# Batch 6's key turn one step sooner, tile 6's token sums split around a PSUM sum, and GpSimd's last value-fold steps held behind them

## The chip, the cores and the metric

The kernel runs on one core of a Trainium2 chip. The metric is device time in microseconds of one execution. The kernel before took 225.37 us (median of three runs, 225.24 to 225.75). The engines are called by the profile's names: PE (matrix multiply), PEld (its weight loads), DVE (vector), ACT (scalar), POOL (GpSimd) and SP (the queue that issues most transfers late in the kernel). Each has a queue of its own, which it works through in program order; semaphores join them.

## The reference

```python
k_p = k.reshape(B, H, Sp, 8, D).mean(axis=3)        # B=8, H=8, S=576, D=64, Sp=72
v_p = v.reshape(B, H, Sp, 8, D).mean(axis=3)
attn = softmax(q @ k_p^T / sqrt(D))
x = (attn @ v_p) as 4608 tokens x 512
h = maximum(maximum(x @ w1, x @ w2), x @ w3)        # 512 -> 768
out = h @ w_out                                     # 768 -> 512
```

## The kernel before, in words

The maximum is taken as x·w1 + max(0, x·(w2-w1), x·(w3-w1)). The part x·w1·w_out is folded into one 512x512 matrix (`wm`), so that the two differences alone are multiplied out, and the output is x·wm + max(...)·w_out.

The work is laid out by batch and by tile. A batch (0 to 7) is 576 tokens of attention: GpSimd sums eight key rows and eight value rows into one, in three steps each (`fold_steps`, L163, L164, L166); PE turns the pooled keys into a PSUM tile `pkt` (`turn_k`, L201), from which four copies (L210) write the two key matrices `kz`, for batches over 2 two by DVE and two by ACT; PE makes scores (L220), ACT their exponentials (L225), PE multiplies with the pooled values in five chunks of 128 tokens (`values`, L270), and DVE divides each chunk (L276, L278). The chunk is then turned by a DMA transpose, issued from SP, into the token ring `xT` (`turn_x`, L255). A tile (0 to 8) is 512 tokens of that ring. Tile 6 is tokens 3072 to 3583: batch 5 from its token 192 on, and the first chunk of batch 6.

From tile 6 on, the hidden products are made from seven block products instead of eight (`seven`, L763). The tile's tokens are cut into two halves of tokens and two of channels, x0 to x3, and four sums of them are needed: T1 = x1-x0, T2 = x3-T1, T3 = x3-x1, T4 = x2-T2 (`fold_t`, L566). DVE makes them for tile 6, in four instructions of 128x512 elements, GpSimd for tile 7. Products 1 and 2 use x0 and x2, product 6 uses T2, product 5 T1, product 7 T3, product 4 T4. A product's result is copied from PSUM by ACT (L805) or added to a kept one by DVE (`plus`, L776: one operand from PSUM).

The order is written out by hand in strings of words. `MIDDLE[4]` (L907) is the middle stage with tile 4's output products, batch 5's value chunks and batch 6's keys; `block(5, LEAD, ...)` follows it, with tile 5's hidden products (L364) and batch 6's scores between them; then `ORDER` (L856) weaves the rest. In `MIDDLE[4]` a word such as `v4` is batch 5's value chunk 4, `x4` its transpose, `6:k` the turn of batch 6's keys, `3` or `2h` an output product (L721), `e5` and `e2` a DVE sum of it into the output (L734), and `k7+3` or `v7+3` three steps of a fold on GpSimd. In `ORDER`, `k7` is batch 7's key turn, `1a` product 1 for the first 128 hidden columns, `F` half an output tile (L414 or L418), `T` the token sums, `v62` batch 6's value chunk 2 and `s70` a piece of batch 7's scores. Every word puts its instructions on all the queues that it needs, so a word that moves, moves on each of them.

Buffers set waits too. The two scores of a piece need both key matrices. `psc`, `pav` and `pkt` share two PSUM slots in the middle stage; `pw` and the output products `oB` and `oC` share three. In the last stage `pkt`, `pB` and `psf` share two (`SC`), `pA` has two, `po` one and `val` one. Tile 6's sums are written to `pad`, whose memory is that of batch 7's value rows `vt`, which the fold's first step reads last. `held` with `gate` (L834) makes the next GpSimd step wait for a DVE instruction.

Of the kernel before, what the change touches and what calls it, by code (L numbers as in the profile page):

```python
# [10 lines left out]
ALU = mybir.AluOpType  # L11
# [3 lines left out]
def kernel(  # L15
# [46 lines left out]
    def psum(shape, dtype, name, tag, bufs):  # L62
        return pools[-1].tile(shape, dtype, name=name, tag=tag, bufs=bufs)
# [3 lines left out]
    def after(loads, first):  # L67
        for x in loads:
            tc.add_manual_dep(x.ins, first.ins.name, mybir.DependencyInfo(
                mybir.DependencyClass.Sync, mybir.DependencyReason.DATA),  # L70
                reason="weights first")

    def load_k(b, eng, dtype=F16, parts=1):
        pad = 0 if b == 0 else 32
        kts[b] = (const if b == 0 else ld).tile(
            [96, 6, POOL * D + pad], dtype, name=f"kt{b == 0}", tag=f"kt{b == 0}")[
                :, :, 0:POOL * D].rearrange("p i (j d) -> p i j d", j=POOL)
        src = k[b].rearrange("h s d -> (h s d)").rearrange(
            "(p i j d) -> p i j d", p=96, i=6, j=POOL)
        n = 6 // parts  # L80
        return [eng.dma_start(out=kts[b][:, i:i + n], in_=src[:, i:i + n])
                for i in range(0, 6, n)][-1]

    def load_v(b, eng, dtype=F16, cuts=(0, H)):
        if b == 0:
            vts[0] = ld.tile([96, 4096], dtype, name="vt0", tag="vt")[:, 0:3072].rearrange(
                "p (h i d) -> p h i d", h=H, i=6)
            src = v[0].rearrange("h (p i) d -> p h i d", i=6)
            return [eng.dma_start(out=vts[0][:, h:g], in_=src[:, h:g])
                    for h, g in zip(cuts, cuts[1:])][-1]  # L90
        vts[b] = ld.tile([Sp, H, POOL, D], dtype, name="vt", tag="vt")
        src = v[b].rearrange("h (sp j) d -> sp h j d", j=POOL)
        return [eng.dma_start(out=vts[b][:, h:g], in_=src[:, h:g])
                for h, g in zip(cuts, cuts[1:])][-1]
# [30 lines left out]
    for sign in (1, -1):  # L125
        nc.gpsimd.affine_select(
            out=pick, in_=pick, compare_op=ALU.is_ge, fill=0.0, base=7 * (sign < 0),
            pattern=[[sign, 6], [-8 * sign, 128]], channel_multiplier=6 * sign)
    for i in range(3):
        load_w(slice(256 * i, 256 * i + 256))  # L130
    nc.gpsimd.dma_start(
        out=wo_sb, in_=moe_w_out.rearrange("(jc p) c -> p jc c", p=128))
# [243 lines left out]
    def new_hT():  # L376
        return sb2.tile([128, JCH, NB], F16, name="hT", tag="hT")
# [178 lines left out]
    def halves(n):  # L556

        return {i: tokens(NB * n + HALF * (i % 2), NB * n + HALF * (i % 2) + HALF,
                          2 * (i // 2), 2 * (i // 2) + 2) for i in range(4)}

    def turns(n):
        return (pad3 if n % 2 else pad)[:, 0:4]

    def fold_t(e, x, t):
        for i, a, b in ((0, x[1], x[0]), (1, x[3], t[0]), (2, x[3], x[1]), (3, x[2], t[1])):
            e.tensor_tensor(out=t[i], in0=a, in1=b, op=ALU.subtract)  # L566

    def fold_x(n):

        x, t = halves(n), turns(n)  # L570
        late = n >= LAST - 1
        for part in ([slice(0, 1), slice(1, 2)] if late else [slice(0, 2)]):
            fold_t(nc.gpsimd if late else nc.vector,
                   {i: x[i][:, part] for i in x}, [t[:, i, part] for i in range(4)])
        return {f"T{i + 1}": t[:, i] for i in range(4)}

    LAST = TOK // NB - 1
    th, so_new, tt_all, gate, held = {}, [], [], [], []
# [184 lines left out]
    def seven(n):  # L763

        x, banks, done = halves(n), {}, set()
        low = pad4[:, 0:2]

        def kept(i, g):
            odd = (3 * n + g) % 2
            return (pad3[:, 4] if odd else pad2[:, 0]) if i == 1 else pad[:, 2 * (i - 3) + odd]  # L770

        def top(g):
            return pad4[:, 2:4] if (3 * n + g) % 2 else pad2[:, 1:3]

        def plus(out, i, g, p):
            nc.vector.tensor_tensor(out=out, in0=kept(i, g), in1=p, op=ALU.add)  # L776

        def best(row, c):
            nc.vector.scalar_tensor_tensor(
                out=hTs[n][:, row, :].rearrange("p (a c) -> p a c", a=2), in0=c[:, :, 0, :],  # L780
                scalar=0.0, in1=c[:, :, 1, :], op0=ALU.max, op1=ALU.max)

        def product(i, g):
            if i == 0:
                x.update(fold_x(n))
                return
            if not done:
                hTs[n] = (ld.tile([128, JCH, NB], F16, name="hT8", tag="ktFalse")
                          if n == LAST else new_hT())
            of = "B" if i == 2 else "C" if i in (4, 7) else "A"  # L790
            if i in FIRST:
                tag = {"A": PA, "B": SC, "C": BC}[of]
                banks[of, g] = psum([128, 2, HALF], F32, name=f"p{of}", tag=tag[0],
                                    bufs=tag[1])
            p = banks[of, g]
            for w in range(2):
                a, b = sw[w + 1][PRODUCTS[i][0]], x[PRODUCTS[i][1]]
                for kc in range(2):
                    mm = nc.tensor.matmul(p[:, w], a[:, kc, bass.ts(g, 128)], b[:, kc, :],  # L799
                                          start=(i in FIRST and w + kc == 0),  # L800
                                          stop=(w + kc == 2), skip_group_check=True)
            mms.append(mm)
            done.add((i, g))
            if i in (1, 6, 5):
                nc.scalar.copy(out=kept(i, g), in_=p)  # L805
            if i == 2:
                plus(top(g)[:, 0], 1, g, p)
            elif i == 3:
                nc.scalar.copy(out=top(g)[:, 1], in_=p)
                best(g, top(g))  # L810
            elif i == 4:
                plus(low[:, 0], 6, g, p)
                best(g + JH, low)
            elif i in (5, 7) and (12 - i, g) in done:
                plus(low[:, 1], 5, g, banks["C", g])

        return product
# [16 lines left out]
    def pool_step(n, name):  # L834

        what, b = name[0], int(name[1])
        if name[2:] == "<":
            load = {"k": lambda: load_k(b, nc.gpsimd), "v": lambda: load_v(b, nc.gpsimd),
                    "q": lambda: load_q(b)}[what]
            op = load()  # L840
            if what == "k":
                after([op], mms[-1])
            return
        if (what, b) not in folding:
            if what == "k":
                new_kp(b)
                folding[what, b] = fold_steps(nc.gpsimd, kts[b], kps[b])
            else:
                folding[what, b] = fold_steps(nc.gpsimd, vts[b], vp_all[:, b, :, 0:D])
        for _ in range(int(name[3:] or 3)):  # L850
            op = next(folding[what, b])
            for x in held:
                after([op], x)
            held.clear()

    ORDER = """  # L856
        k7 1a F F 2a T 1b v62 s70 F s71 s72 6a F s73 v63 5a 7a s74 s75 v64 F s76
        4a s77 3a s78 6b 2b 7b 1c v70 2c 5b T F 6c v71 3b F 5c 4b F v72 7c 3c 1a
        F 1b 4c v73 2a 2b 6b 6a F v74 5a 7a F 3a F T 1c 4a 5b 2c 6c 7b 3b F 5c
        4b F 1a 7c 2a 3c 6a 4c H 1b 2b 5a 6b 7a 3a h o1 1c 4a o2 5b 6c 7b 2c o6  # L860
# [3 lines left out]
    def weave():  # L864

        products, seen = {}, {}
        for name in ORDER.split():
            if name == "F":
                next(tiles)
            elif name == "H":  # L870
                fold_h(LAST - 1)
                outs = out_seven(LAST - 1)
            elif name == "h":
                fold_h(LAST - 1, True)
            elif name[0] == "o":
                outs(int(name[1]), 0, 1)
            elif name[0] in "ksvx":
                b = int(name[1])
                do(b, name[0] + name[2:])
                if name[0] == "v" and b > 2:  # L880
                    do(b, "x" + name[2:])
                if name[0] == "s" and name[2] == "4" and b + 1 < B:
                    do(b + 1, "T")
            else:
                n = seen[name] = seen.get(name, 5) + 1
                if n not in products:
                    products[n] = seven(n)
                products[n](*((0, 0) if name == "T" else
                              (int(name[0]), "abc".index(name[1]))))

    MIDDLE = {
        1: """
# [14 lines left out]
        4: """  # L907
            h k k7< q7< v7< h a1 a3 a2 a4 f ! v5+2 h h s0 h s1 h s2 h s3 h s4 b1 f ! k6+1 h s5
            h s6 h s7 h b2 b3 b4 f ! k6+2 v6+1
            1 v0 x0 2l v1 x1 7:T 6 7 v2 x2 5 v3 x3 e5 v4 x4 2h 3 6:k e2 4 v6+2 k7+3 v7+3  # L910
        """}
    folds = iter([f for wi in range(1, 3) for f in [fold_w(wi)] * 4])

# [81 lines left out]
```

## Time and profile before

| | |
|---|---|
| median of the runs | 225.37 us (225.24 to 225.75) |
| the profiled execution | 225.68 us |
| its span, first to last instruction | 224.0 us |
| PE busy | 214.2 us, 96% of the span |
| PEld, DVE, ACT, POOL busy | 146.6, 149.4, 122.4, 140.1 us |
| granted PE clock | 0.999 |
| chain that ended last | PE 86%, DVE 5%, DMA 3%, ACT 2% |

The profile is of one execution; its 224.0 us of span and 1.7 us around it make its 225.68 us. A row of the timeline has the start in us from the span's start, how long it lasts, engine, line, operation, output and inputs by the program's names, shape and how many instructions were merged; a bracket gives the idle time before it and what ended that. Matmuls are pipelined: a row's length holds the drain of its last one, so that the next row starts before it ends. A PE instruction's own share is read from the starts.

### The profile page before, as it was taken

How to read it: one execution, taken by the hardware profiler on the slowest of the kernel's cores; microseconds unless marked ns; L12 is line 12 of the kernel's file. 1: busy time of each engine (PE TensorE's matmuls, PEld its weight loads, DVE VectorE, ACT ScalarE, POOL GpSimd, SP SyncE). 2: the span in 40 equal slices, each digit the busy share in tenths (PEclk: the TensorE clock that was granted, in tenths of full speed). 3: DMA queues.
4: the chain of work that ended last, by engine and by line, in shares of the span. 5: the costliest groups of instructions: out<-in, count | busy, mean ns of one | idle time of the engine just before them, and what ended most of it. 6: DMA issues, size and time to landing. Idle time of an engine off the chain costs nothing.

```text
span 224.0 us, 4682 instructions
## 1 busy us (share of the span) xinstructions
PE 214.2 (96%) x1806; PEld 146.6 (65%) x1807; DVE 149.4 (67%) x292; ACT 122.4 (55%) x221; POOL 140.1 (63%) x111
## 2 busy tenths in 40 slices
PE   7688999999999999999999999999999999999993
PEld 2377744558755555875596569555587777788882
DVE  3558967037594395787479668727677786898840
ACT  2267534766875478237723862583876446554330
POOL 7975300999949977787768757999601903772020
PEclk9999999999999999999999999999999999999999
DMA  6999999989849999839999999764341523200266
GB/s 176 211 197 197 204 207 205 205 161 213 158 105 154 237 202 228 135 79 170 225 234 168 165 248 150 160 170 77 66 101 31 128 61 84 47 3 0 63 200 164
DMA packets 50710, 33.54 MB, mean 150 GB/s; under 512 B 27040, under 2 KB 46368, under 8 KB 50688
## 3 DMA queue, kind: packets, MB, share of 16 engines
q0 software_dynamic: 20304, 16.98, 48.3%
q1 hardware_dynamic: 29936, 15.87, 31.8%
q10 hardware_dynamic: 448, 0.39, 0.7%
q8 instruction: 14, 0.23, 0.5%
q14 instruction: 8, 0.07, 0.1%
HBM read 34.60 MB, written 9.44 MB: 197 GB/s over the span
## 4 chain that ended last, share of the span: by engine, by line
PE 86%; DVE 5%; DMA 3%; ACT 2%; issue 1%; SPq 0%; DVEq 0%; ACTq 0%
PE pw L364 26%; PE po L418 9%; PE oA L721 9%; PE pA L799 7%; PE psc L220 6%; PE po L414 5%; PE oC L721 4%; PE pav L270 4%; PE pC L799 4%; DMA ktTrue<-in_k_dram 3%; PE pm L351 2%; PE oB L721 2%; PE pxt L261 2%; PE pB L799 2%; PE pqt L194 1%; DVE xn L278 1%
## 5 line engine op out<-in xcount | busy, mean ns | idle before, releaser
L364 PE MATMUL pw<-xT,mw 128*128 128x512 f16 (+1 forms) x336 | 72.8, 348 | 0.3 <-ACT xT L264 0.2
L364 PEld LDWEIGHTS <-mw 128*128 128x128 f16 x336 | 31.6, 98 | 20.4 <-issue 0.6
L372 DVE TENSOR_TENSOR hT<-t,pw 128x512 f16<-128x512 f16 (+1 forms) x42 | 25.4, 610 | 23.2 <-ACT et L225 14.9
L225 ACT ACTIVATE et<-psc 72x576 f16<-72x576 f32 (+2 forms) x54 | 35.2, 661 | 6.7 <-PE psc L220 6.6
L163 POOL TENSOR_TENSOR half<-vt 72x2048 f32<-72x2048 f16 x7 | 28.4, 4059 | 13.7 <-DMA vt<-in_v_dram 13.3
L164 POOL TENSOR_TENSOR half<-half 72x1024 f32<-72x1024 f32 (+1 forms) x13 | 27.3, 2099 | 10.7 <-DVE rcp L276 6.1
L370 ACT ACTIVATE t<-pw 128x512 f16<-128x512 f32 (+1 forms) x42 | 22.6, 537 | 14.8 <-PE pw L364 14.3
L278 DVE TENSOR_TENSOR xn<-pav,rcp 128x512 f16<-128x512 f32 x40 | 27.7, 692 | 1.4
L220 PE MATMUL psc<-qT,kz 128*128 128x320 bf16 (+2 forms) x120 | 22.6, 278 | 1.3 <-DVE qT L196 0.9
L418 PE MATMUL po<-mwo,hT 128*128 128x512 f16 (+1 forms) x102 | 23.5, 366 | 0.0
L220 PEld LDWEIGHTS <-kz 128*128 128x128 bf16 x143 | 13.1, 98 | 13.8 <-ACT qT L196 1.1
L163 POOL TENSOR_TENSOR half<-ktFalse 96x1536 f32<-96x1536 f16 x6 | 18.8, 3131 | 4.0 <-issue 2.9
L805 ACT CAST pad<-pA 128x512 f16<-128x512 f32 x27 | 15.6, 588 | 7.4 <-PE pA L799 7.2
L566 POOL TENSOR_TENSOR pad<-xT 128x256 f16<-128x256 f16 x8 | 5.9, 738 | 20.8 <-ACT pad L805 12.2
L276 DVE RECIPROCAL rcp<-pav 128x8 f32<-128x8 f32 x40 | 8.2, 204 | 15.2 <-PE pav L270 14.9
L270 PEld LDWEIGHTS <-et 72*128 72x128 f16 x320 | 15.2, 98 | 3.5 <-issue 0.2
L731 ACT COPY osb<-oA 128x512 f32<-128x512 f32 x12 | 7.0, 586 | 18.2 <-PE oA L721 18.2
L414 PE MATMUL po<-wm,xT 128*128 128x512 f16 (+1 forms) x68 | 16.6, 366 | 0.0
L270 PE MATMUL pav<-vp,et 72*128 72x65 f16 x320 | 16.4, 194 | 0.1
L423 ACT COPY osb<-po 128x512 f32<-128x512 f32 (+1 forms) x16 | 9.2, 573 | 12.3 <-PE po L418 12.3
L799 PEld LDWEIGHTS <-sw 128*128 128x128 f16 x144 | 13.7, 98 | 3.0 <-issue 0.6
L776 DVE TENSOR_TENSOR pad<-pad,pC 128x512 f16<-128x512 f16 x18 | 12.3, 685 | 3.9 <-PE pC L799 3.6
(122 smaller groups left out, 383.4 us busy)
## 6 DMA issues: line engine op xcount, KB each, us to landing
out_dram<-osb SPq DMA_DIRECT2D x38, 128.0 KB, 5.2
ktFalse<-in_k_dram POOLq DMA_DIRECT2D x7, 576.0 KB, 8.4
qb<-in_q_dram POOLq DMA_DIRECT2D x7, 576.0 KB, 12.6
vt<-in_v_dram POOLq DMA_DIRECT2D x7, 576.0 KB, 16.7
mw<-in_moe_w_dram POOLq DMA_DIRECT2D x9, 256.0 KB, 9.4
out_dram<-osb SPq DMA_DIRECT2D x8, 256.0 KB, 6.1
ktTrue<-in_k_dram SPq DMA_DIRECT2D x3, 384.0 KB, 5.1
out_dram<-ob SPq DMA_DIRECT2D x8, 128.0 KB, 2.7
```

What stands on the lines that cost most here:

```text
L163: yield e.tensor_tensor(out=f, in0=t[:, :, 0:4, :], in1=t[:, :, 4:8, :], op=ALU.add)
L164: yield e.tensor_tensor(out=f[:, :, 0:2, :], in0=f[:, :, 0:2, :], in1=f[:, :, 2:4, :], op=ALU.add)
L220: nc.tensor.matmul(out, kz_all[b % 2][f % 2][rows, h, :], qTs[b][rows, n + i0:n + i1, 64 * (h % 2):64 * (h % 2) + 64], start=True, stop=True)
L225: nc.scalar.activation(out=out, in_=in_, func=FT.Exp, scale=1.0 / 64.0)
L270: nc.tensor.matmul(pav[:, h // 4, 65 * (h % 4):65 * (h % 4) + 65], ets[b][:, h, c0:c0 + 128], vp_all[:, b, h, :], start=True, stop=True)
L278: nc.vector.tensor_tensor(out=xn, in0=pv[:, :, :, 0:D], in1=rcp.to_broadcast([128, 2, 4, D]), op=ALU.mult)
L364: mm = nc.tensor.matmul(pw, w_sb[wi][:, kc, bass.ts(jc, 128)], x[:, kc], start=(kc == 0), stop=(kc == KCH - 1))
L372: nc.vector.tensor_tensor(out=hT[:, jc, c0:c1], in0=t, in1=pw, op=ALU.max)
L414: nc.tensor.matmul(po, tokens(128 * m, 128 * m + 128)[:, kc], wm_sb[:, kc, c], start=(kc == 0), stop=False)
L418: nc.tensor.matmul(po, hT[:, jc, bass.ts(mm, 128)], wo_sb[:, jc, c], start=False, stop=(jc == JCH - 1))
L721: nc.tensor.matmul(p, left, right, stop=(r == 4), skip_group_check=True, start=(i in FIRST and r == 0 and (m == 0 or n == LAST)))
L799: mm = nc.tensor.matmul(p[:, w], a[:, kc, bass.ts(g, 128)], b[:, kc, :], start=(i in FIRST and w + kc == 0), stop=(w + kc == 2), skip_grou ...
```

## The change

Two places of the written order are changed, and two helpers so that the token sums can be made in two parts.

- `MIDDLE[4]`: `v4 x4 2h 3 6:k` becomes `2h 6:k 3 v4 x4`. The key turn of batch 6 now stands ahead of output product 3 and of batch 5's value chunk 4; that chunk and its transpose stand behind product 3 and the stores which that product issues. `v7+3` at the end becomes `v7+1`.
- `ORDER`: `k7 1a F F 2a T 1b` becomes `1a k7 F F T 2a U 1b`. Product 1a stands ahead of batch 7's key turn. `T` makes only T1 and T2 for tile 6, ahead of product 2a and its `plus`; `U` makes T3 and T4 behind it. `U` then holds GpSimd's last two steps of batch 7's value fold (`v7+2`) until T4 is made.

```diff
-    def fold_t(e, x, t):
-        for i, a, b in ((0, x[1], x[0]), (1, x[3], t[0]), (2, x[3], x[1]), (3, x[2], t[1])):
-            e.tensor_tensor(out=t[i], in0=a, in1=b, op=ALU.subtract)
-
-    def fold_x(n):
+    def fold_t(e, x, t, which=(0, 1, 2, 3)):
+        for i in which:
+            a, b = ((x[1], x[0]), (x[3], t[0]), (x[3], x[1]), (x[2], t[1]))[i]
+            gate[:] = [e.tensor_tensor(out=t[i], in0=a, in1=b, op=ALU.subtract)]
+
+    def fold_x(n, rest):
 
         x, t = halves(n), turns(n)
         late = n >= LAST - 1
+        which = (0, 1, 2, 3) if late else (2, 3) if rest else (0, 1)
         for part in ([slice(0, 1), slice(1, 2)] if late else [slice(0, 2)]):
             fold_t(nc.gpsimd if late else nc.vector,
-                   {i: x[i][:, part] for i in x}, [t[:, i, part] for i in range(4)])
+                   {i: x[i][:, part] for i in x}, [t[:, i, part] for i in range(4)], which)
...
             if i == 0:
-                x.update(fold_x(n))
+                x.update(fold_x(n, g))
...
     ORDER = """
-        k7 1a F F 2a T 1b v62 s70 F s71 s72 6a F s73 v63 5a 7a s74 s75 v64 F s76
+        1a k7 F F T 2a U 1b v62 s70 F s71 s72 6a F s73 v63 5a 7a s74 s75 v64 F s76
...
-                products[n](*((0, 0) if name == "T" else
+                products[n](*((0, name == "U") if name in "TU" else
                               (int(name[0]), "abc".index(name[1]))))
+                if name == "U":
+                    held[:] = gate
+                    pool_step(n, "v7+2")
...
-            1 v0 x0 2l v1 x1 7:T 6 7 v2 x2 5 v3 x3 e5 v4 x4 2h 3 6:k e2 4 v6+2 k7+3 v7+3
+            1 v0 x0 2l v1 x1 7:T 6 7 v2 x2 5 v3 x3 e5 2h 6:k 3 v4 x4 e2 4 v6+2 k7+3 v7+1
```

## The prediction

> **What bounds the kernel now.** I read the page first: PE is busy for 96% of the span and holds 86% of the chain that ended last, at a granted clock of 0.999. A change that adds and removes no matmul can pay only where PE stands still. So I read the waits of the stretch that the change touches (130 to 180 us). Columns: who waited for whom, us in total, times, longest.
>
> ```profile
> PE pA L799 <- DVE pad L566: 0.5, 1, 0.5
> PE psc L220 <- ACT kz L210: 0.3, 1, 0.3
> DVE pad L776 <- ACT pad L805: 1.9, 2, 1.7
> ```
>
> PE waits twice: once for a token sum, once for a key copy. Next PE's timeline there, for the size of both.
>
> ```profile
> 142.62 0.30 PE L220 MATMUL psc<-qT,kz 128*128 128x320 bf16 x1
> 143.20 0.28 PE L220 MATMUL psc<-qT,kz 128*128 128x256 bf16 x1 [0.28 <-ACT kz L210]
> 144.18 0.41 PE L220 MATMUL psc<-qT,kz 128*128 128x320 bf16 x2
> 144.42 1.03 PE L364 MATMUL pw<-xT,mw 128*128 128x512 f16 x4
> ...
> 159.99 0.60 PE L220 MATMUL psf<-qT,kz 128*128 128x64 bf16 x6
> 161.07 0.60 PE L799 MATMUL pA<-pad,sw 128*128 128x256 f16 x4 [0.47 <-DVE pad L566]
> ```
>
> The brackets are too short, because a row's length holds its pipeline's drain. By starts, a pair of scores takes 144.42 - 144.18 = 0.24 us for 576 columns, so its first 320 take 0.13: the second score could have started at 142.76 and started at 143.20, a gap of **0.44**. The next pw group starts 0.86 to 0.87 us after a pw group of four 512-column matmuls, so the six score pieces (1024 columns) take 0.43: product 6a could have started at 160.42 and started at 161.07, a gap of **0.65**. Worked the same way, starts show no other gap of PE over 0.05 us from 100 us to its last matmul at 220. After 161.07 PE is thus the clock of the rest, and what it saves here it keeps, if no other engine is late.
>
> Then the engines that PE waited for: DVE, ACT and POOL.
>
> ```profile
> 140.52 0.69 DVE L278 TENSOR_TENSOR xn<-pav,rcp 128x512 f16<-128x512 f32 x1
> 141.12 0.96 DVE L210 COPY kz<-pkt 64x288 bf16<-64x288 bf16 x2
> 142.12 0.69 DVE L734 TENSOR_TENSOR osb<-osb,oB 128x512 f32<-128x512 f32 x1
> ...
> 158.59 0.69 DVE L776 TENSOR_TENSOR pad<-pad,pB 128x512 f16<-128x512 f16 x1 [1.70 <-ACT pad L805]
> 159.19 0.42 DVE L566 TENSOR_TENSOR pad<-xT 128x512 f16<-128x512 f16 x1
> 159.65 1.37 DVE L566 TENSOR_TENSOR pad<-xT,pad 128x512 f16<-128x512 f16 x1
> 160.94 0.41 DVE L566 TENSOR_TENSOR pad<-xT 128x512 f16<-128x512 f16 x1
> ```
> ```profile
> 142.18 0.96 ACT L210 COPY kz<-pkt 64x288 bf16<-64x288 bf16 x2 [0.86 <-DVE kz L210]
> ...
> 156.98 0.97 ACT L210 COPY kz<-pkt 64x288 bf16<-64x288 bf16 x2 [1.99 <-DVE kz L210]
> 157.97 0.59 ACT L805 CAST pad<-pA 128x512 f16<-128x512 f32 x1
> ```
> ```profile
> 152.77 4.06 POOL L163 TENSOR_TENSOR half<-vt 72x2048 f32<-72x2048 f16 x1
> 156.91 2.36 POOL L164 TENSOR_TENSOR half<-half 72x1024 f32<-72x1024 f32 x1
> 159.35 1.39 POOL L166 TENSOR_TENSOR vp<-half 72x512 f16<-72x512 f32 x1
> ```
>
> First gap: batch 6's key copies stand on DVE behind chunk 4's division; ACT's pair starts only when DVE's pair is done and ends at 143.14. Second gap: DVE stood idle for 1.70 us, because `plus` of 2a waited for ACT's cast of 1a, itself behind ACT's two key copies; the token sums stood behind `plus`; and T2 then took 1.37 where T3 and T4 took 0.41, while POOL's L166 ran (159.35 to 160.74).
>
> **The change, part by part.** No instruction is added or taken away; all are moved.
>
> *6:k ahead of 3 and v4.* On PE the three `pkt` transposes go from 140.53 to behind 2h: product 5 ends at 138.37, v3 takes 0.26, 2h 0.55, so 139.18. POOL's `kp` (137.66 for 0.99) is done at 138.65: cover of 0.5 us; each us later than that would stall PE. DVE's copies then follow e5's sum (139.69, next start 140.28) and end at 141.25; ACT's pair runs 141.3 to 142.3 instead of 142.18 to 143.14. The score that waited until 143.20 wants to start at 142.76: the gap of 0.44 closes, with 0.45 to spare. PE's order of 3, v4 and 4 keeps its sum.
>
> What is late next? On ACT the copy of product 3 now stands behind the key copies, 142.3 instead of 140.73; the relu copy behind it starts at 142.8 (143.16 before), its input being done at about 142.8. On DVE, chunk 4's division moves behind the key copies, so e2's sum of `oB` still starts at 142.12 and ends at 142.81; the second pw group takes oB's PSUM slot and, with the gap gone, wants to start at 142.86. That is the tightest place: the trace shows 0.05 us from a DVE end to PE's start (161.02 to 161.07). Bounds: no wait, or at the worst the whole 0.44 if DVE slips. I take 0, the nearest row being e2's own unchanged start. Scores s0 take `pkt`'s slot, free at 142.3, wanted at 142.62.
>
> On SP, the two stores of product 3 (0.68 each of the four that take 3.08, waits included) go ahead of x4, which is issued near 146.9 instead of 145.5. Its landing, 2.2 to 3.5 us after (rows of this stretch), is at about 150; T1 wants it at 157. Nothing, unless it takes 8 us more.
>
> *1a ahead of k7.* On PE 1a's 0.44 and the 0.13 of `pkt` change places. With PE 0.44 earlier, 1a ends at 155.05 and ACT casts it at 155.2 instead of 157.97; DVE's key copies end near 156.5, ACT's near 157.5. The first score of batch 7 takes `pkt`'s slot at 158.47 instead of 158.91: covered by 1 us.
>
> *T ahead of 2a's plus.* T1 now needs three things: DVE free (156.5), batch 6's first chunk in `xT` (transpose issued at 153.36, median 3.7 to landing in that stretch, so 157.06, or 156.6 if it moves with PE), and the memory of `vt`, which POOL's first v7 step leaves at 156.83. T1 starts at about 157, T2 ends at 157.8, 0.41 each. PE has 2a done at 157.8; `plus` runs 157.9 to 158.6 (158.59 to 159.28 before). It frees the slot of s71, which PE wants at 159.55: cover 0.9 us. 6a wants T2 at 159.98: cover 2.2 us. **The gap of 0.65 closes.**
>
> *U, then v7+2.* T3 and T4 run to 159.4; 7a needs T3 only at 162.6 (163.72 before, less 1.09) and 4a T4 later. Behind U, chunk v62's division runs from 159.4 (161.62 before). POOL starts its last two steps at 159.5 instead of 156.91 and ends after 2.36 + 1.39 at 163.3 (160.74 before). Queued behind them on POOL are tile 7's sums (172.91); the waiter is v70, at 169.00 before, 167.9 now: cover of 4.6 us. DVE's next instructions with both inputs in SBUF (L779) start at 166.2, so the fold's later place meets none.
>
> **Sum:** -0.44 - 0.65 = -1.09 us. The profiled execution of 225.68 us (span 224.0 and 1.7 around it) would become 224.59; it lies 0.31 above the median of the runs, so the median becomes 225.37 - 1.09 = **224.28**.
>
> **The rivals.**
>
> *A: only the second gap closes.* DVE or ACT slips around e2's sum, and PE waits for `oB` at 142.86 instead of for a key copy. For it: no slack there. Against it: DVE's chain has the same instructions in front. 225.37 - 0.65 = 224.72.
>
> *B: only the first gap closes*, because 6a meets another wait, such as ACT's exponentials, whose slots s72 needs: ACT had only 0.40 us of idle before them. 225.37 - 0.44 = 224.93.
>
> *C: slower.* T1 now stands at the head of DVE's queue, ahead of `plus`, and waits there for the DMA transpose of batch 6's first chunk; `plus` holds the slot of s71, and s71 stands ahead of 6a on PE. No loss up to T1 at 158.1; from a start at 159.2 the change loses, that is from a landing 6.3 us after the issue at 152.92. The longest of the 27 such transposes took 9.0: then T1 starts at 161.95, `plus` ends 1.39 later, 6a starts at 163.83 instead of 161.07, and the time is 225.37 + 2.76 = 228.1. Against it: 3.7 here, with the DMA engines lightly loaded.
>
> *D: the hold doesn't hold.* If POOL's second v7 step started at 156.91 as before, just ahead of T1, T1 would wait for its end, as T2 waited 0.96 us beside L166. T1 would then start at 159.3 and T2 meet L166 as it did before and end at 161.0; `plus` would end at 161.6 instead of by 159.5, and s71 would be late by 2.1 us: 225.37 - 1.09 + 2.1 = 226.4. Against it: the code makes that step wait for T4.
>
> The Trainium skill, page "SBUF — State Buffer", section "Who interferes with whom", has the rule for this: a DVE instruction with two SBUF inputs and a GpSimd instruction that reads SBUF exclude each other, and the later one waits for the whole of the earlier. T2's 1.37 us agree. By that rule the order of T and the value fold without the hold gives D's 226.4; if the two only slowed each other in passing, T2's 0.96 alone would be lost, 6a would keep its cover of 2.2 us and the hold would be worth nothing.
>
> **How the numbers follow.** Forecast 0.76, A 0.08, B 0.04, C 0.05, D 0.02, and 0.05 for the gain given back at a later wait that I have not seen, which comes out near 225.4. A difference of 0.2% (0.45 us) is about what a measurement of this kernel can tell from none. Faster: 0.76 + 0.08 + 0.04 = 0.88; same 0.05; slower, C and D, 0.07. The range holds the forecast, A and B: up to 224.93 with 0.2 for the spread of runs (225.24 to 225.75), so 225.1; down to 224.28 less 0.28 of the same spread, 224.0, as there is no third gap to win.
>
> **What would show it.** Right: after, PE has no wait for `kz` near 142.8 and none for `pad` near 160; ACT's L210 ends near 142.3; both L566 of T1 and T2 stand ahead of L776, at 0.41 each; POOL's L164 starts after T4. Wrong: a wait of pw for DVE's `osb` near 142.9 (A), of pA or psf for ACT (B), a DVE L566 that waits for DMA with psf behind it (C), or a new gap in PE after 165 that eats the gain.

## The result and the profile after

| | before | after |
|---|---|---|
| median of 18 runs | 225.70 us (225.03 to 226.30) | 224.47 us (224.18 to 225.38) |
| the profiled execution | 225.68 us | 224.89 us |
| its span | 224.0 us | 223.2 us |

The ratio of the two is 0.9947, with a 95% interval of 0.9936 to 0.9959: 1.2 us less (0.9 to 1.4). The forecast was -1.09 us. The median of before over 18 runs is 0.33 us above that of the first three, so that the forecast's 224.28 stands against 224.47.

PE's timeline after, at the two places. Columns here and in the timelines below: start and length in us, engine, line, operation, tiles and shape, count, and in a bracket the idle time before it and what ended it. From L562 on, the changed kernel's lines are one to five higher than before: the token sums are L567, `plus` L778, the products L801, ACT's casts L807.

```profile
142.91 0.41 PE L220 MATMUL psc<-qT,kz 128*128 128x320 bf16 x2
143.15 1.02 PE L364 MATMUL pw<-xT,mw 128*128 128x512 f16 x4
...
159.83 0.60 PE L220 MATMUL psf<-qT,kz 128*128 128x64 bf16 x6
160.27 0.60 PE L801 MATMUL pA<-pad,sw 128*128 128x256 f16 x4
```

The two scores stand together, and the next pw group starts 0.24 us after them. Product 6a starts 0.44 us after the six score pieces, which is their own time. Both brackets are gone. By starts, PE has no gap over 0.05 us from 100 us to its last matmul, where it had two that added up to 1.08 (0.44 and 0.64; the prediction rounded the second to 0.65).

The span shows 0.8 us of this. In this execution PE is already 0.27 us later when product 5 ends (138.64 against 138.37), which is ahead of both places (PE waited 0.50 us for GpSimd's `kp` near 55.6, where the profile of before has no such gap); 6a comes 0.80 earlier (160.27 against 161.07), and 0.80 + 0.27 = 1.07.

DVE after, at both places:

```profile
140.55 0.97 DVE L210 COPY kz<-pkt 64x288 bf16<-64x288 bf16 x2
142.40 0.68 DVE L736 TENSOR_TENSOR osb<-osb,oB 128x512 f32<-128x512 f32 x1
...
156.64 0.73 DVE L567 TENSOR_TENSOR pad<-xT 128x512 f16<-128x512 f16 x1
157.40 0.43 DVE L567 TENSOR_TENSOR pad<-xT,pad 128x512 f16<-128x512 f16 x1
158.32 0.69 DVE L778 TENSOR_TENSOR pad<-pad,pB 128x512 f16<-128x512 f16 x1 [0.49 <-PE pB L801]
158.93 0.42 DVE L567 TENSOR_TENSOR pad<-xT 128x512 f16<-128x512 f16 x1
```

The key copies end at 141.52 (142.08 before), e2's sum of `oB` at 143.08, and T2 at 157.83 instead of 161.02, in 0.43 us instead of 1.37. T1 took 0.73, beside GpSimd's first step. ACT and GpSimd after:

```profile
141.89 0.97 ACT L210 COPY kz<-pkt 64x288 bf16<-64x288 bf16 x2 [2.46 <-DVE rcp L276]
155.53 0.58 ACT L807 CAST pad<-pA 128x512 f16<-128x512 f32 x1 [0.70 <-PE pA L801]
```
```profile
153.03 4.05 POOL L163 TENSOR_TENSOR half<-vt 72x2048 f32<-72x2048 f16 x1
159.82 2.34 POOL L164 TENSOR_TENSOR half<-half 72x1024 f32<-72x1024 f32 x1 [2.74 <-DVE rcp L276]
162.24 1.27 POOL L166 TENSOR_TENSOR vp<-half 72x512 f16<-72x512 f32 x1
```

GpSimd stands still for 2.74 us between its first and second step, until T4 is made (159.68; the bracket names the reciprocal that DVE ran next, but the step's wait in the program is for T4). Its third then takes 1.27, where it took 1.39 beside the token sums. Nobody waits for its later end at 163.51.

### The profile page after: what moved, and what is told of

Its sections match the earlier page's. It is cut to its first block, busy times and chain, and to the rows that moved or that the text cites. A ratio compares the mean times of both kernels' runs of the same rounds, so it can differ in the third digit from the quotient of the medians.

```text
span 223.2 us, 4680 instructions
## 1 busy us (share of the span) xinstructions
PE 214.5 (96%) x1807; PEld 146.6 (66%) x1807; DVE 149.6 (67%) x292; ACT 122.2 (55%) x221; POOL 140.1 (63%) x111
## 4 chain that ended last, share of the span: by engine, by line
PE 72%; DMA 13%; POOL 11%; issue 1%; DVE 0%; ACTq 0%; ACT 0%; POOLq 0%
PE pw L364 22%; PE oA L723 10%; DMA vt<-in_v_dram 8%; PE pA L801 7%; PE po L418 6%; PE oC L723 4%; PE psc L220 4%; PE po L414 4%; DMA mw<-in_moe_w_dram 4%; PE pC L801 4%; PE pav L270 4%; POOL half L163 3%; PE oB L723 2%; POOL half L164 2%; PE pB L801 2%; POOL mw L110 1%
## 5 line engine op out<-in xcount | busy, mean ns | idle before, releaser
L372 DVE TENSOR_TENSOR hT<-t,pw 128x512 f16<-128x512 f16 (+1 forms) x42 | 25.4, 608 | 22.8 <-ACT et L225 16.4
L807 ACT CAST pad<-pA 128x512 f16<-128x512 f32 x27 | 15.5, 587 | 8.2 <-PE pA L801 8.1
L567 POOL TENSOR_TENSOR pad<-xT 128x256 f16<-128x256 f16 x8 | 5.8, 721 | 16.8 <-ACT pad L807 8.6
L781 DVE SCALAR_TENSOR_TENSOR hT<-pad 128x512 f16<-128x512 f16 x18 | 13.9, 785 | 2.1 <-ACT pad L811 1.7
L801 PEld LDWEIGHTS <-sw 128*128 128x128 f16 x144 | 13.7, 98 | 2.4
```

The costliest lines, as they stand in the source:

```text
L372: nc.vector.tensor_tensor(out=hT[:, jc, c0:c1], in0=t, in1=pw, op=ALU.max)
```

## The experiments

Times are ratios to the kernel before, run beside each on the same chip. The "gaps" are those of PE from 100 us on, worked out from starts as in the prediction, in the one profiled execution of each kernel.

| run | edit | ratio, 95% interval | gaps, us |
|---|---|---|---|
| the change | all | 0.9947, 0.9936 to 0.9959 | 0 |
| after_again | all, beside the last three | 0.9951, 0.9933 to 0.9969 | 0 |
| m_alone | middle stage alone | 0.9982, 0.9959 to 1.0006 | 0.99 |
| m_again | the same | 0.9992, 0.9974 to 1.0011 | 0.99 |
| o_alone | all but the middle stage | 0.9964, 0.9948 to 0.9981 | 0.45 |
| hold_alone | the hold alone | 0.9964, 0.9946 to 0.9982 | 0.45 |
| swap_alone | 1a ahead of k7 alone | 1.0002, 0.9988 to 1.0016 | 1.03 |
| no_hold | all but the hold | 0.9976, 0.9959 to 0.9993 | 0.82 |
| plus_first | all but T ahead of 2a | 0.9958, 0.9943 to 0.9974 | 0 |
| k7_first | all but the swap | 0.9954, 0.9934 to 0.9974 | 0 |
| late_x0 | all, T1's input late | 0.9985, 0.9973 to 0.9998 | 0.66 |
| min_two | middle stage and hold | 0.9944, 0.9926 to 0.9962 | 0.26 |
| k2_later | all, batch 2's key turn later | 0.9935, 0.9914 to 0.9956 | 0 |

### The middle stage alone

```diff
-            1 v0 x0 2l ... e5 v4 x4 2h 3 6:k e2 4 v6+2 k7+3 v7+3
+            1 v0 x0 2l ... e5 2h 6:k 3 v4 x4 e2 4 v6+2 k7+3 v7+3
```

> The kernel before with the middle stage's new order alone (6:k ahead of product 3 and chunk 4); the last stage and the value fold stay. Theory (two separate gaps of PE): the wait of 0.44 us for the key copy is gone, the wait of 0.65 us for T2 stays: -0.44 us, a ratio near 0.998. Rival A (PE waits for oB in its place): 0. Rival that the two gaps depend on each other (an earlier PE only waits longer at T2, since GpSimd's fold does not move): also 0, with a gap near 1.1 at 6a.

This run's interval (0.9959 to 1.0006) is too wide to choose between -0.44 and 0. The trace chooses. Its waits of PE from 130 to 180 us, DVE's sums and GpSimd's fold:

```profile
PE pA L799 <- DVE pad L566: 0.8, 1, 0.8
```
```profile
158.63 0.77 DVE L566 TENSOR_TENSOR pad<-xT 128x512 f16<-128x512 f16 x1
159.43 1.37 DVE L566 TENSOR_TENSOR pad<-xT,pad 128x512 f16<-128x512 f16 x1
```
```profile
156.76 2.35 POOL L164 TENSOR_TENSOR half<-half 72x1024 f32<-72x1024 f32 x1
159.19 1.33 POOL L166 TENSOR_TENSOR vp<-half 72x512 f16<-72x512 f32 x1
```

The wait for the key copy is gone, and the one at 6a has grown from 0.64 to 0.99. PE comes sooner, but GpSimd's fold keeps its own pace: T1 now waits for the end of the second step as well, T2 for that of the third. Of 0.44 us won, 0.35 are given back. The same edit was run again with this as the theory:

> The middle stage's new order alone, once more. The first such run showed PE's gap at 6a grown from 0.64 to 0.99 us. Theory now (T2's end hangs on GpSimd's fold, which does not move with PE): the gaps after 100 us add up to about 1.0 again, so -0.1 us, ratio near 0.9996. Rival (the first trace was an odd one, the gaps are independent): a gap of 0.64 at 6a, -0.44 us, ratio near 0.998.

The gap at 6a was 0.99 again, and the ratio 0.9992. The prediction had the two gaps as independent, and they are not: the first is worth about 0.1 us alone in PE's gaps, and the whole 0.44 only once the second is closed.

### The last stage alone, and the hold alone

For o_alone the changed kernel keeps the middle stage's old order, with `v7+1`. For hold_alone, moreover:

```diff
-        1a k7 F F T 2a U 1b v62 ...
+        k7 1a F F 2a T U 1b v62 ...
```

> The changed kernel with the middle stage's old order: only 1a ahead of k7, T, U and the hold. Theory: the wait for T2 is gone and that for the key copy stays at 0.44: -0.65 us, a ratio near 0.997. Rival: -1.1, if the earlier key turn was worth nothing.

> The kernel before with one thing: GpSimd's last two steps of batch 7's value fold wait for T4. k7 stays ahead of 1a and all four sums behind the plus of 2a. Theory (the T2 gap is T2's exclusion by GpSimd's L166): T1 to T4 run from 159.2 at 0.42 each, T2 ends near 160.0, before PE wants it at 160.4, so this alone closes the gap: -0.65 us. Rival (the gap is the late place of the sums, behind plus and ACT's cast): the gap stays at least in part, 0 to -0.3.

Both came out at 0.9964 (-0.8 us; -0.4 to -1.2), with the key copy's gap alone left, at 0.45. PE's waits in hold_alone, then its DVE:

```profile
PE psc L220 <- ACT kz L210: 0.3, 1, 0.3
```
```profile
158.52 0.69 DVE L778 TENSOR_TENSOR pad<-pad,pB 128x512 f16<-128x512 f16 x1 [1.69 <-ACT pad L807]
159.12 0.42 DVE L567 TENSOR_TENSOR pad<-xT 128x512 f16<-128x512 f16 x1
159.57 0.42 DVE L567 TENSOR_TENSOR pad<-xT,pad 128x512 f16<-128x512 f16 x1
```

DVE still idles 1.69 us for ACT's cast, and the sums still stand behind `plus`. With GpSimd still, they take 0.42 each, T2 ends at 159.99, and PE takes it at 160.37. So the hold alone closes the second gap.

### The swap alone, and each of the two cover moves undone

swap_alone has `1a k7 F F 2a T 1b` in the kernel before. In the changed kernel, plus_first has `1a k7 F F 2a T U 1b`, and k7_first `k7 1a F F T 2a U 1b`.

> The kernel before with 1a ahead of k7 alone. Theory: the plus of 2a comes 0.5 us sooner, T1 then waits for GpSimd's second step (to 159.3) and T2 for its third, so T2 ends near 161.0 as before: 0 us. Rival (the gap comes from the late cast): -0.5 to -0.65.

> The changed kernel with T behind 2a, so that all four sums stand behind the plus of 2a again; the hold, 1a ahead of k7 and the middle stage stay. Theory: T2 ends near 159.8, before PE wants it near 160.1, so the place of T ahead of the plus is worth nothing once GpSimd is held: -1.1 us. Rival (the place carries the second gap): -0.44.

> The changed kernel with k7 ahead of 1a again; T, U, the hold and the middle stage stay. Theory: ACT's cast of 1a comes 2.4 us later, plus ends near 159.0, and s71 wants its slot only near 159.6: -1.1 us, nothing lost. Rival: plus ends too late and s71 waits, -0.6 or worse.

The swap alone moves nothing: 1.0002, T2 again 1.38 us, gaps of 0.45 and 0.58. Undoing either move in the changed kernel opens no gap, and 0.9958 and 0.9954 are not to be told from 0.9947. In k7_first `plus` ended at 159.04 without s71 waiting for its slot:

```profile
157.46 0.42 DVE L567 TENSOR_TENSOR pad<-xT,pad 128x512 f16<-128x512 f16 x1
158.35 0.69 DVE L778 TENSOR_TENSOR pad<-pad,pB 128x512 f16<-128x512 f16 x1 [0.46 <-ACT pad L807]
```

### Without the hold

The middle stage ends with `v7+3` again, and the two lines behind `U` are taken out:

```diff
-                if name == "U":
-                    held[:] = gate
-                    pool_step(n, "v7+2")
```

> The changed kernel without the hold: v7+3 stands in the middle stage as before, U does T3 and T4 only. Theory (exclusion for a whole instruction): T2 waits for the 2.36 us of GpSimd's second step, plus comes behind it, and PE waits for the slot of s71: against the kernel before between -0.3 us (T1 gets in ahead of that step) and +1.0 us (T1 waits for it too). Rival (the two only slow each other in passing): -1.1, as the changed kernel.

DVE, GpSimd and PE of no_hold:

```profile
155.65 0.73 DVE L567 TENSOR_TENSOR pad<-xT 128x512 f16<-128x512 f16 x1
156.41 2.47 DVE L567 TENSOR_TENSOR pad<-xT,pad 128x512 f16<-128x512 f16 x1
158.92 0.69 DVE L778 TENSOR_TENSOR pad<-pad,pB 128x512 f16<-128x512 f16 x1
159.53 0.77 DVE L567 TENSOR_TENSOR pad<-xT 128x512 f16<-128x512 f16 x1
```
```profile
156.17 2.43 POOL L164 TENSOR_TENSOR half<-half 72x1024 f32<-72x1024 f32 x1
158.68 1.33 POOL L166 TENSOR_TENSOR vp<-half 72x512 f16<-72x512 f32 x1
```
```profile
159.66 0.60 PE L220 MATMUL psf<-qT,kz 128*128 128x64 bf16 x6 [0.65 <-DVE pad L778]
```

T1 got in ahead of the second step, T2 didn't: 2.47 us for an instruction of 0.42. `plus` stood behind it, and s71 came 0.82 us late, waiting for the PSUM slot. The gap moved from 6a to s71. The ratio of 0.9976 (-0.5 us) is worse than the change's, their intervals touching at 0.9959. The rule of the Trainium skill weighed in the prediction ("SBUF — State Buffer", "Who interferes with whom") agrees: T2 lost nearly the whole of the other instruction (2.05 of 2.43 us), and did not merely run slower for a while.

### T1's input late

```diff
-            8: [(6, "v0 x0")], 9: [(6, "v1 x1")]}
+            8: [(6, "v0")], 9: [(6, "v1 x1 x0")]}
```

> The changed kernel with the transpose of batch 6's first chunk issued behind that of its second (1.5 to 2 us later), so that T1, at the head of DVE's queue, waits for it. It tests rival C's price. Theory: the chunk lands near 158.5 to 159, T1 starts there, plus ends 1.4 us later, and s71 waits for its slot: 0.4 to 0.9 us of the gain are lost, -0.2 to -0.7 us against the kernel before. Rival (there is more cover than reckoned): -1.1.

```profile
158.31 0.42 DVE L567 TENSOR_TENSOR pad<-xT 128x512 f16<-128x512 f16 x1 [2.10 <-DMA xT<-xn]
158.77 0.43 DVE L567 TENSOR_TENSOR pad<-xT,pad 128x512 f16<-128x512 f16 x1
159.23 0.69 DVE L778 TENSOR_TENSOR pad<-pad,pB 128x512 f16<-128x512 f16 x1
```
```profile
159.97 0.60 PE L220 MATMUL psf<-qT,kz 128*128 128x64 bf16 x6 [0.50 <-DVE pad L778]
```

T1 waited 2.10 us at the head of DVE's queue, and PE lost 0.66 at s71. So rival C is a true mechanism, and this is the one cost that the new place of T carries: by the order of the queue, with T behind `plus` the slot would not wait for a transpose (not run). The time from T1's start to the end of `plus` is 1.61 us, where the prediction had reckoned 1.39.

### The two edits that carry it, and one more gap

min_two is the kernel before with the middle stage's new order and the hold, and `k7 1a F F 2a T U 1b`. k2_later is the changed kernel with, in `MIDDLE[1]`:

```diff
-            h q4< k4< v4< h 1:x2 h 1:v4 h 1:x3 h h 1:x4 h k h q0 h h q1 ...
+            h q4< k4< v4< h 1:x2 h 1:v4 h 1:x3 h h 1:x4 h h k q0 h h q1 ...
```

> The kernel before with two edits alone: the middle stage's new order and GpSimd's hold behind T4. k7 stays ahead of 1a, and all four sums stay behind the plus of 2a. Theory (the hold closes the second gap, the key turn the first, and the rest of the change is cover): no gap of PE left after 100 us, -1.1 us, ratio near 0.995. Rival (the swap or the place of T is needed once PE comes 0.44 us sooner): a gap of 0.1 to 0.5 us stays at 6a or s71.

> The changed kernel itself, beside the others on the same chip: ratio near 0.995, no gap of PE over 0.05 us after 100 us.

> The changed kernel with batch 2's key turn one hidden piece later in the first middle stage. In the changed kernel PE waits 0.50 us there for GpSimd's kp; a piece of 0.44 us takes its place. Theory (a gap of PE closed ahead of dense work is time won, wherever it is): -0.4 us more than the changed kernel, ratio near 0.993. Rival (the copies of the keys, 2 us on DVE, only shift a wait to the next pieces, or GpSimd's fixed pace takes it back later): as the changed kernel, 0.995.

min_two came out at 0.9944 and has neither old gap. The times alone do not part it from hold_alone (0.9926 to 0.9962 against 0.9946 to 0.9982); PE's gaps do. The 0.26 that it shows is elsewhere, ahead of tile 5's first product, which wants the DMA transpose of batch 5's chunk 1. The issue line of that transpose, with us from issue to landing at the end:

```profile
xT<-xn SPq DMA_TRANSPOSE x1, 4.1
```

It was issued at 138.10, as in the profile of after, where it took 3.6; 4.1 ends at 142.2, PE started at 142.29 and could have started 0.26 sooner, at 142.03. This place is in every version, and in the profile of after it had about 0.3 us to spare (landed at 141.66, PE started at 142.03).

k2_later has the lowest median (224.31 us, 0.9935), but its interval holds after_again's 0.9951. The 0.50 us at GpSimd's `kp`, for which it was made, turned out to differ between executions: the changed kernel's first profile had it, m_alone's, k7_first's and swap_alone's had 0.29, 0.43 and 0.43, and the others, after_again's too, had none. What k2_later's trace shows closed is another gap, of 0.30 us a little later (0.06 left): a hidden product waits for a PSUM slot whose reader on DVE (L372) stands behind the 2 us of copies of the same keys. So it is the best candidate, not a shown gain.

## Why the prediction was right, point by point

- **Two gaps of PE, and dense work behind them.** Shown: 1.08 us of gaps before and none after, and a time that fell by 1.2 (0.9 to 1.4). Nothing was given back after 165.
- **The key turn sooner.** The gap closed with less to spare than worked out. DVE's pair ended at 141.52 against 141.25 forecast, in a profile that is 0.27 late. ACT's pair ended at 142.86 against 142.3 (142.6 with that), and the second score wanted it at 143.04: 0.18 us to spare instead of 0.45. It began 0.37 us after DVE's pair, behind chunk 4's reciprocal, where it had begun 0.10 after; what held it is not shown. The tightest place, e2's sum, had 0.07 us where 0.05 was reckoned, and rival A did not come.
- **The two terms added.** Here the working failed, though the sum was right. The first term stands at 0.44 only because the second edit is there; alone it is 0.09 in gaps (1.08 to 0.99). So rival B's 224.93 was mis-sized: with the first gap alone closed, T2's end stays with GpSimd's fold, and the wait grows.
- **What closes the second gap.** The prediction named three causes (the cast behind the key copies, the sums behind `plus`, T2 beside GpSimd's step) and put the gain under T's new place. hold_alone shows that the third is enough; swap_alone shows that removing the first cause alone is worth nothing. T's place and the swap were cover that nobody needed: min_two has neither.
- **D's price.** The mechanism was right and its size was not: the term of 2.1 us measured 0.82, since T1 slipped in between GpSimd's steps, so that DVE lost one step and not two ahead of `plus`.
- **C's threshold.** Right in kind, and 0.2 us too generous.
- **T1's start.** T2's end was forecast for 157.8 and measured at 157.83, partly by luck. The prediction had T1 wait until 156.83 for the memory of batch 7's `vt`. That wait does not exist: T1's row starts while GpSimd's first step still reads those rows (156.64 against an end at 157.08; in no_hold 155.65 against 156.09). Built, the kernel has `pad` in the memory of batch 6's value rows, and `pad3`, tile 7's, in that of batch 7's. T1 was kept out by that first step all the same, as T2 was by the third, and by nearly the time that the memory would have cost. `plus` ended at 159.01 against 158.6, since product 2a was done at 158.21 and not at 157.8; s71 started at 159.83, so 0.8 us of cover was left. The fold ended at 163.51 against 163.3.

## What to carry to other kernels

A bracket in the timeline names who ended a wait, not what made that one late: T2's 1.37 us beside others of 0.41 said more than the place of T in the queue. When two waits stand in a row on one engine, ask whether the second one's source moves with the engine; if it doesn't (here GpSimd's fold), closing the first only lengthens the second, and the two are worth their sum only together. Of the change's four parts (the middle stage's order, the swap, T's place, the hold), two carried all the gain; undoing each in turn, and then running the two alone, showed which.

## What the runs showed of the hardware

These are DVE's token sums, with both inputs in SBUF, beside GpSimd's fold steps. In the program T2 and T3 wait for no instruction of GpSimd. A DVE sum kept out by GpSimd shows no idle time: its row begins when it is at the head and is as long as its wait. Its end stands 0.28 to 0.29 us after the end of the GpSimd step beside it, every time that rows here let it be read: T2 before (161.02 and 160.74), T1 after (157.37 and 157.08), T2 in no_hold (158.88 and 158.60), T3 in no_hold (160.30 and 160.01), T1 and T2 in m_alone (159.40 and 159.11, 160.80 and 160.52). The waiting sum gets in before GpSimd's next step, and that step then keeps out the next sum: with both queues full they took turns here, so that a sum of 0.42 us took up to the whole of a GpSimd step (2.47 us in no_hold, beside a step of 2.43).
